# Vector engine instructions in written order from tile 36 on, in an attention and feed-forward kernel

## The chip, the cores and the metric

The kernel runs on one core of one Trainium2 chip. The metric is the device time of one execution in microseconds (us). A core has engines that run side by side, each with its own queue of instructions: TensorE for matmuls and transposes (PE in the profile, with its weight loads as PEld), VectorE (DVE), ScalarE (ACT), GpSimd (POOL) and SyncE (SP), which here issues all DMA transfers. An engine takes its queue from front to back; an instruction that has to wait for another engine holds up what stands behind it in the same queue.

## The reference

```python
# q, k, v: [8, 8, 576, 64]; w_in: [512, 2048]; w_out: [2048, 512]
scores = scale * q @ k.T
thresh = max(scores, axis=-1) - tau
scores = where(scores >= thresh, scores, -1e9)
attn   = exp(scores - max(scores))
attn   = attn / (sum(attn) + 1e-9)
x      = attn @ v                      # heads side by side: [4608, 512]
h      = x @ w_in
out    = (max(h, 0) + log1p(exp(-abs(h)))) @ w_out
```

So it is an attention whose weights below a threshold are dropped, followed by a two-layer feed-forward with softplus between the layers. The matrix products are made in several passes: numbers are split into a high part, rounded to the matmul's format, and a low part, the rest.

## The kernel before

**Tiles.** One unit is one batch with a pair of heads, 32 units in all. A unit has nine tiles of 128 query rows, so there are 288 tiles; the main loop (L924) goes through them one after another. Tiles 0 to 35 are batch 0, and tile 36 is the first of batch 1. A tile of scores is 128 x 576 numbers and lies in one of two pairs of PSUM banks (`SB = 2`).

**A tile's chain.** TensorE makes the scores (L423). DVE takes the negated row maximum `negm` (L430) and the threshold `thr` (L431). ACT makes the exponentials into `e_all` (L435). DVE masks them and sums the rows in the same instruction (L440, `mask`). TensorE transposes the result back into the bank of the scores (L471 to L477). ACT copies the high part `gH` (L498 to L510), and DVE subtracts to get the low part `gL` (L523, L527, both through the helper at L132). TensorE multiplies with v (`values`, L555 to L557); DVE adds the two halves of the result (L566, `xp`). At the end of a unit, DVE makes the reciprocals of the row sums (L571, L572, `rs`), which TensorE transposes (L576, `rT`).

**Feed-forward beside it.** The 4608 rows of x go through the feed-forward in nine chunks of 512. The matmuls of a chunk (L645 to L649 for h, L703 to L707 for the output) are handed out a few at a time between the steps of the tiles, so that TensorE has them while the chain of a tile runs on other engines. A chunk begins when its batch is through the attention. Two finished blocks of h go together through softplus on ACT (L667), which needs another function table than the exponential, so two table loads stand around each pair. From chunk 1 on DVE rounds the result to the high part (L129, `CAST g<-st`, through `hi_of` at L688); POOL subtracts for the low part (L132 on POOL, `g<-st,g`). In chunk 0 ACT does the rounding. The output of 128 rows is made in four quarters of the hidden width, 12 matmuls each; ACT copies the first quarter to `acc` (L718) and DVE adds the other three (L720, `acc<-o,acc`). The blocks of h and o, the products with v, the transposed queries and keys and `rT` share four PSUM banks (`GB = 4`), so a bank is free again only when its reader is done.

**Weights.** w_in and w_out are brought from 64-bit words into 32-bit parts on the core, 32 pieces, one about every two tiles, so from tile 0 to some time after tile 62. A piece is loaded by DMA (L185), goes through ACT (L193) and POOL (L194), then through three integer instructions on DVE (L200, L202, L205, `second`), then POOL. Where there is room (`took > 1`, the pieces named `wa_`), these steps are deferred by some points and each stands behind a mask (`behind(i, masked)`). Where there is none (`took` 0 or 1, the pieces named `ws_`), `later_` calls each step at once, so the three DVE instructions are written directly after the DMA's issue.

**What sets the order.** The code writes a tile's steps by the letters of `PAT`:

```python
PAT = "ThRlefmpfxSvwp"
```

T is the transposes of tile t, h its high parts, R the row maximum of tile t+1, l the low parts of tile t, e the exponentials of t+1, f feed-forward matmuls, m the mask of t+1, x steps of the units beside it, S the scores of t+2, w the next piece of the weights. At p (`point`) the deferred functions that are due are written: softplus one point after its h is complete, the rounding one point after softplus, the sum `acc` and the sum `xp` one point after their matmuls. The written order isn't the order of the queues: when the program is built, the framework's list scheduler lays out each engine's queue with its own estimate of every duration. Among the instructions that it holds for ready it takes the one written first, so an instruction that is ready early goes ahead of one written earlier that still waits. Softplus has a raised priority (`SPP = 150`). `behind(i, others)` adds an edge without a semaphore: it only tells the scheduler that `i` comes after the last of `others`.

Of the kernel before, what the change touches and what calls it, by code (L numbers as in the profile page):

```python
# [59 lines left out]
def tile_kernel(ctx: ExitStack, tc: tile.TileContext, q, k, v, tau, w_in, w_out, out):  # L60
# [89 lines left out]
    def to_f32(src, want, name, then):  # L150
# [47 lines left out]
        def second(n):  # L198
            if n == 0:
                i = nc.vector.tensor_scalar(out=mu, in0=mu, scalar1=3, scalar2=None, op0=ALU.logical_shift_left)  # L200
            elif n == 1:
                i = nc.vector.scalar_tensor_tensor(out=mu, in0=high, scalar=0x80000000, in1=mu,  # L202
                                                   op0=ALU.bitwise_and, op1=ALU.bitwise_or)
            else:
                i = nc.vector.scalar_tensor_tensor(out=mu, in0=low, scalar=29, in1=mu,  # L205
                                                   op0=ALU.logical_shift_right, op1=ALU.bitwise_or)
# [168 lines left out]
    def queries(s, t0, t1, ps):  # L375

        nc.scalar.activation(t0, ps, AF.Copy, scale=qscale)
        if s.i:
            swap(t0, t1)
            return  # L380
        for i, o in ((slice(0, D), slice(D, P)), (slice(D, P), slice(0, D))):
            nc.vector.tensor_scalar(out=t1[o], in0=ps[i], scalar1=qscale[i], scalar2=None, op0=ALU.mult)
# [44 lines left out]
    def row_max(s, t):  # L427
        negm = apool.tile([P, 1], F32, tag="negm", bufs=3, name=f"negm_{s.i}_{t}")
        thr = apool.tile([P, 1], F32, tag="thr", bufs=3, name=f"thr_{s.i}_{t}")
        nc.vector.reduce_max(negm, s.sp[t][:, :, 0:HS], axis=AX.XY, negate=True)  # L430
        nc.vector.tensor_scalar(out=thr, in0=negm, scalar1=-1.0, scalar2=ntau, op0=ALU.mult, op1=ALU.add)  # L431
        s.m[t] = (negm, thr)
# [5 lines left out]
    def mask(s, t):  # L438
        e2 = e_all[:, s.half[t], :].rearrange("p (h n) -> p h n", h=2)
        masked.append(nc.vector.scalar_tensor_tensor(  # L440
# [76 lines left out]
    def weights_lo(s, t):  # L517
# [3 lines left out]
        for g, c0, s0, n in s.place[t]:  # L521
            h, l = group(s, g)
            lo_of(nc.vector, l[:, :, c0:c0 + n], main[:, :, s0:s0 + n], h[:, 0:NC, c0:c0 + n])  # L523
        for x, rows, up, down in rests(s, t):
            for g, c0, s0, n in s.place[x]:
                h = group(s, g)[0]
                lo_of(nc.vector, h[down, NC, c0:c0 + n], rest[rows, s0:s0 + n], h[up, NC, c0:c0 + n])  # L527
# [32 lines left out]
    def values_out(s, g, o):  # L560
# [5 lines left out]
        nc.vector.tensor_tensor(out=xs, in0=o[keep, 0:n], in1=xs, op=ALU.add)  # L566

    def row_scales(s):
        nt = len(s.tiles)
        s.rs = apool.tile([P, 9], F32, tag="rs", name=f"rs_{s.i}")  # L570
        nc.vector.tensor_scalar(out=s.rs[:, 0:nt], in0=s.sums[:, 0:nt], scalar1=1e-9, scalar2=None, op0=ALU.add)  # L571
        nc.vector.reciprocal(s.rs[:, 0:nt], s.rs[:, 0:nt])  # L572
# [104 lines left out]
    def parts_of(u, fc, t):  # L677
# [10 lines left out]
        hi_of(nc.vector if u.n else nc.scalar, gh, t)  # L688
# [23 lines left out]
    def project_out(u, qt, tb, o):  # L712
# [4 lines left out]
        if qt == 0:  # L717
            nc.scalar.copy(a, o)  # L718
        else:
            nc.vector.tensor_tensor(out=a, in0=o, in1=a, op=ALU.add)  # L720
# [66 lines left out]
    now = {"p": 0}  # L787
# [114 lines left out]
    eng, u0.eng, u0.eng_lo = u0.eng, nc.scalar, nc.vector  # L902
# [21 lines left out]
    for g, (cur, t) in enumerate(tiles):  # L924
        t9 = cur.tiles.index(t) + 1
# [73 lines left out]
```

## Time and profile before

| | |
|---|---|
| median of the runs | 1450.6 us (1448.82, 1451.17, 1450.6) |
| profiled execution | 1451.43 us, of which the span is 1449.6 us |
| busy over the span | PE 1398.8, DVE 987.2, ACT 847.1, POOL 590.3 us |
| masks (L440) | 288 of 816 ns |
| row maxima (L430) | 288 of 754 ns |
| roundings (L129) | 128 of 485 ns |
| sums of the output (L720) | 108 of 689 ns |

The profile names an instruction by its line, engine, and output<-inputs. A timeline row is start, duration, engine, line, operation, names, shapes, count, and in brackets the idle time before it with the engine that ended it. A row of waits is the waiting engine and instruction, the engine and instruction waited for, the microseconds in total, how often, and the longest. In a table of windows each engine has its busy time and its number of instructions in that stretch; PEclk is the clock that TensorE was granted, as a share of full speed.

### The profile page before, as it was taken

Reading aid. Unit: us, or ns where it says so; the run is one execution under the profiler, and the core shown is the slowest. Engines: PE = TensorE matmul, PEld = TensorE weight load, DVE = VectorE, ACT = ScalarE, POOL = GpSimd, SP = SyncE. Lnnn points to the kernel's source line nnn. Section 1 sums busy time; section 2 is a strip of 40 time slices with the busy share of each in tenths; the row PEclk is TensorE's granted clock in tenths of the full one; section 3 lists DMA queues with packets and bytes.
Section 4 is the critical chain, followed back from the end, with each engine's and each line's share of the span. In section 5 each row is a group of like instructions: output and inputs, shape, how many; then the busy total and the mean of one; then the engine's idle time right before and its main releaser. Section 6 shows DMA issues by size and latency. Waiting matters only on the chain.

```text
span 1449.6 us, 23487 instructions
## 1 busy us (share of the span) xinstructions
PE 1398.8 (96%) x7860; PEld 1161.8 (80%) x7860; DVE 987.2 (68%) x2211; ACT 847.1 (58%) x1615; POOL 590.3 (41%) x619
## 2 busy tenths in 40 slices
PE   6887999999999999999999999999999999999998
PEld 4555688788888888888888888888888888788886
DVE  6988588787777777777777777777777777402111
ACT  6667667667656576657665665667665765311010
POOL 3667566443333333344334333344334431324221
PEclk9999999999999999999999999999999999999999
DMA  5866765445333533445433533354344432333321
GB/s 170 227 186 206 214 191 182 126 121 160 104 106 114 135 109 116 119 132 151 122 111 96 154 105 100 117 151 120 113 119 135 147 99 73 105 126 130 118 86 44
DMA packets 131208, 189.93 MB, mean 131 GB/s; under 512 B 35312, under 2 KB 86800, under 8 KB 131088
## 3 DMA queue, kind: packets, MB, share of 16 engines
q1 hardware_dynamic: 131088, 188.43, 44.5%
q8 instruction: 63, 1.03, 0.3%
q14 instruction: 57, 0.47, 0.1%
HBM read 140.51 MB, written 27.41 MB: 116 GB/s over the span
## 4 chain that ended last, share of the span: by engine, by line
PE 78%; DVE 8%; ACT 4%; issue 3%; DMA 3%; POOL 3%; SPq 1%; POOLq 0%; DVEq 0%; ACTq 0%
PE s L423 10%; PE h L647 9%; PE h L645 9%; PE h L649 8%; PE o L707 8%; PE o L705 8%; PE o L703 8%; PE s L474 7%; PE pv L555 3%; PE pv L556 3%; PE tr L364 2%; DVE e_all L440 2%; DVE negm L430 2%; POOL g L132 1%; DMA wc_i<-in_moe_w_in_dram 1%
## 5 line engine op out<-in xcount | busy, mean ns | idle before, releaser
L132 POOL TENSOR_TENSOR g<-st,g 128x512 fp32r<-128x512 f32 x144 | 191.6, 1348 | 195.6 <-DVE g L129 184.2
L440 DVE SCALAR_TENSOR_TENSOR e_all<-s,thr,e_all 128x576 f32<-128x576 f32 x288 | 234.6, 816 | 49.1 <-ACT e_all L435 45.8
L430 DVE TENSOR_REDUCE negm<-s 128x1 f32<-128x576 f32 x288 | 217.2, 754 | 43.5 <-PE s L423 36.0
L707 PE MATMUL o<-wo_o,g 128*128 128x512 f32 x576 | 232.5, 404 | 5.3 <-POOL g L132 5.3
L435 ACT ACTIVATE e_all<-s,negm 128x576 f32<-128x576 f32 x288 | 216.0, 750 | 33.5 <-PE tr L471 14.8
L647 PE MATMUL h<-xl,wi 128*128 128x512 f32 x576 | 233.9, 406 | 0.9 <-POOL xl L132 0.9
L703 PE MATMUL o<-wo_o,g 128*128 128x512 f32 x576 | 232.3, 403 | 0.8 <-DVE acc L720 0.4
L645 PE MATMUL h<-xh,wi 128*128 128x512 f32 x576 | 230.6, 400 | 2.3 <-ACT xh L127 2.0
L649 PE MATMUL h<-xh,wi 128*128 128x512 f32 x576 | 230.6, 400 | 0.0
L705 PE MATMUL o<-wo_o,g 128*128 128x512 f32 x576 | 228.4, 397 | 0.0
L498 ACT CAST gH<-s 128x512 fp32r<-128x512 f32 (+1 forms) x270 | 145.1, 550 | 140.6 <-PE s L474 137.8
L132 DVE TENSOR_TENSOR gL<-s,gH 128x512 fp32r<-128x512 f32 (+1 forms) x270 | 169.0, 634 | 46.4 <-ACT gH L498 24.0
L423 PE MATMUL s<-kT,qT 128*128 128x288 f32 x1024 | 193.1, 310 | 7.6 <-ACT gH L512 2.0
L423 PEld LDWEIGHTS s<-kT,qT 128*128 128x128 f32 x1024 | 149.3, 191 | 28.2 <-issue 10.8
L129 DVE CAST g<-st 128x512 fp32r<-128x512 f32 x128 | 57.4, 485 | 149.5 <-ACT st L667 149.0
L474 PE MATMUL s<-identr,e_all 128*128 128x128 f32 x1008 | 154.6, 276 | 3.9 <-DVE e_all L440 3.9
L667 ACT ACTIVATE st<-h 128x512 f32<-128x512 f32 x144 | 78.3, 596 | 115.6 <-PE h L649 115.0
L707 PEld LDWEIGHTS o<-wo_o,g 128*128 128x128 f32 x576 | 108.4, 188 | 29.2 <-POOL g L132 11.0
L474 PEld LDWEIGHTS s<-identr,e_all 128*128 128x128 f32 x1008 | 114.8, 141 | 20.7 <-DVE e_all L440 12.5
L645 PEld LDWEIGHTS h<-xh,wi 128*128 128x128 f32 x576 | 108.9, 189 | 26.1 <-ACT xh L127 2.6
L647 PEld LDWEIGHTS h<-xl,wi 128*128 128x128 f32 x576 | 108.9, 189 | 23.2 <-POOL xl L132 1.7
L649 PEld LDWEIGHTS h<-xh,wi 128*128 128x128 f32 x576 | 109.0, 189 | 21.9
(107 smaller groups left out, 2363.4 us busy)
## 6 DMA issues: line engine op xcount, KB each, us to landing
wi<-wi_d SPq DMA_DIRECT2D x144, 512.0 KB
qT<-qT SPq DMA_DIRECT2D x124, 128.0 KB
R<-r_d SPq DMA_DIRECT2D x64, 144.0 KB
kn<-in_k_dram SPq DMA_DIRECT2D x32, 256.0 KB
qn<-in_q_dram SPq DMA_DIRECT2D x32, 256.0 KB
vn<-in_v_dram SPq DMA_DIRECT2D x32, 256.0 KB
wc_i<-in_moe_w_in_dram SPq DMA_DIRECT2D x16, 512.0 KB
wi_d<-wc_i SPq DMA_DIRECT2D x32, 256.0 KB
```

The source lines that it names most:

```text
L132: eng.tensor_tensor(out=out_, in0=in_, in1=hi.bitcast(F32), op=ALU.subtract)
L423: i = nc.tensor.matmul(sp[:, hf, 0:HS], lhs, s.kT[j][:, k0 + hf * HS:k0 + (hf + 1) * HS], start=(m == 0), stop=(m == len(parts) - 1))
L430: nc.vector.reduce_max(negm, s.sp[t][:, :, 0:HS], axis=AX.XY, negate=True)
L435: nc.scalar.activation(e_all[:, s.half[t], :].rearrange("p (h n) -> p h n", h=2), s.sp[t][:, :, 0:HS], AF.Exp, bias=s.m[t][0], scale=1.0)
L440: masked.append(nc.vector.scalar_tensor_tensor(out=e2, in0=s.sp[t][:, :, 0:HS], scalar=s.m.pop(t)[1], in1=e2, op0=ALU.is_ge, op1=ALU.mult, ...
L474: nc.tensor.matmul(main[:, c, :], e[:, c0:c0 + P], ident, is_transpose=True, start=True, stop=True)
L645: nc.tensor.matmul(h, wi[:, 0, cc, :], u.h[cc], start=(cc == 0), stop=False)
L647: nc.tensor.matmul(h, wi[:, 0, cc, :], u.l[cc], start=False, stop=False)
L649: nc.tensor.matmul(h, wi[:, 1, cc, :], u.h[cc], start=False, stop=(cc == NCC - 1))
L703: nc.tensor.matmul(o, gh[:, sl], wo[fc][:, 0, :], start=(i == 0), stop=False)
L705: nc.tensor.matmul(o, gh[:, sl], wo[fc][:, 1, :], start=False, stop=False)
L707: nc.tensor.matmul(o, gl[:, sl], wo[fc][:, 0, :], start=False, stop=(i == QF - 1))
```

## The change

A class `Queue` wraps the vector engine. From tile 36 on (`now["tile"] >= TG`), every instruction that is issued through it gets an edge without a semaphore behind the one issued before it. All DVE work of the loop goes through the wrapper: row maxima, thresholds, masks, low parts, the sums `xp` and `acc`, reciprocals, roundings and the three steps of the weights. So the DVE queue from there on is the written order, and the scheduler can no longer let one DVE instruction pass another. In it, what is due at the point after a mask stands behind that mask, and ahead of the next row maximum. Nothing is added or removed that runs, no priority is changed, and the queues of the other engines are still laid out by the scheduler, now around another DVE order.

```diff
+    now = {"p": 0, "tile": 0}
...
+    class Queue:
+
+        def __init__(self, eng):
+            self.eng, self.last = eng, []
+
+        def __getattr__(self, name):
+            def call(*args, **kwargs):
+                i = getattr(self.eng, name)(*args, **kwargs)
+                if now["tile"] >= TG:
+                    behind(i, self.last)
+                    self.last = [i]
+                return i
+            return call
+
+    vec = Queue(nc.vector)
...
-                i = nc.vector.tensor_scalar(out=mu, in0=mu, scalar1=3, scalar2=None, op0=ALU.logical_shift_left)
+                i = vec.tensor_scalar(out=mu, in0=mu, scalar1=3, scalar2=None, op0=ALU.logical_shift_left)
...
-        nc.vector.reduce_max(negm, s.sp[t][:, :, 0:HS], axis=AX.XY, negate=True)
+        vec.reduce_max(negm, s.sp[t][:, :, 0:HS], axis=AX.XY, negate=True)
...
-        masked.append(nc.vector.scalar_tensor_tensor(
+        masked.append(vec.scalar_tensor_tensor(
...
-            lo_of(nc.vector, l[:, :, c0:c0 + n], main[:, :, s0:s0 + n], h[:, 0:NC, c0:c0 + n])
+            lo_of(vec, l[:, :, c0:c0 + n], main[:, :, s0:s0 + n], h[:, 0:NC, c0:c0 + n])
...
-        hi_of(nc.vector if u.n else nc.scalar, gh, t)
+        hi_of(vec if u.n else nc.scalar, gh, t)
...
-            nc.vector.tensor_tensor(out=a, in0=o, in1=a, op=ALU.add)
+            vec.tensor_tensor(out=a, in0=o, in1=a, op=ALU.add)
...
     for g, (cur, t) in enumerate(tiles):
+        now["tile"] = g
```

The remaining lines of the diff replace `nc.vector` by `vec` in the same way at L202, L205, L382, L431, L527, L566, L571, L572 and L902.

More of the change, by code (lines that the diff above doesn't have):

```diff
@@ L381, in queries @@
         for i, o in ((slice(0, D), slice(D, P)), (slice(D, P), slice(0, D))):
[L382 removed]
+            vec.tensor_scalar(out=t1[o], in0=ps[i], scalar1=qscale[i], scalar2=None, op0=ALU.mult)
     def swap(t0, t1):
@@ L429, in row_max @@
         thr = apool.tile([P, 1], F32, tag="thr", bufs=3, name=f"thr_{s.i}_{t}")
-        nc.vector.reduce_max(negm, s.sp[t][:, :, 0:HS], axis=AX.XY, negate=True)
-        nc.vector.tensor_scalar(out=thr, in0=negm, scalar1=-1.0, scalar2=ntau, op0=ALU.mult, op1=ALU.add)
+        vec.reduce_max(negm, s.sp[t][:, :, 0:HS], axis=AX.XY, negate=True)
+        vec.tensor_scalar(out=thr, in0=negm, scalar1=-1.0, scalar2=ntau, op0=ALU.mult, op1=ALU.add)
         s.m[t] = (negm, thr)
@@ L526, in weights_lo @@
                 h = group(s, g)[0]
-                lo_of(nc.vector, h[down, NC, c0:c0 + n], rest[rows, s0:s0 + n], h[up, NC, c0:c0 + n])
+                lo_of(vec, h[down, NC, c0:c0 + n], rest[rows, s0:s0 + n], h[up, NC, c0:c0 + n])
     slow, ends = [], []
@@ L565, in values_out @@
         nc.scalar.copy(xs, o[move, 0:n])
-        nc.vector.tensor_tensor(out=xs, in0=o[keep, 0:n], in1=xs, op=ALU.add)
+        vec.tensor_tensor(out=xs, in0=o[keep, 0:n], in1=xs, op=ALU.add)
     def row_scales(s):
@@ L570, in row_scales @@
         s.rs = apool.tile([P, 9], F32, tag="rs", name=f"rs_{s.i}")
-        nc.vector.tensor_scalar(out=s.rs[:, 0:nt], in0=s.sums[:, 0:nt], scalar1=1e-9, scalar2=None, op0=ALU.add)
-        nc.vector.reciprocal(s.rs[:, 0:nt], s.rs[:, 0:nt])
+        vec.tensor_scalar(out=s.rs[:, 0:nt], in0=s.sums[:, 0:nt], scalar1=1e-9, scalar2=None, op0=ALU.add)
+        vec.reciprocal(s.rs[:, 0:nt], s.rs[:, 0:nt])
     def row_scales_T(s):
```

7 lines of the change are left out of this document (3 added, 4 removed).

## The prediction

> **What bounds the kernel now.** First the head of the page, and its chain that ended last.
>
> ```profile
> span 1449.6 us, 23487 instructions
> PE 1398.8 (96%) x7860; PEld 1161.8 (80%) x7860; DVE 987.2 (68%) x2211; ACT 847.1 (58%) x1615; POOL 590.3 (41%) x619
> ...
> PE 78%; DVE 8%; ACT 4%; issue 3%; DMA 3%; POOL 3%; SPq 1%; POOLq 0%; DVEq 0%; ACTq 0%
> ```
>
> TensorE is busy for 96% of the span. The change works on DVE alone, so it can gain only what TensorE still loses to DVE. Where that lies, a table of three stages tells: batch 1, in which the weights are still being prepared; batches 2 to 7; and the two feed-forward chunks at the end.
>
> ```profile
> 145.00:300.00 155.00, 149.44 (x827) 119.25 (x826) 120.89 (x259) 105.05 (x197) 89.49 (x98) 0.98 0.58 170
> 300.00:1250.00 950.00, 939.88 (x5551) 806.47 (x5550) 715.39 (x1646) 614.56 (x1144) 355.41 (x368) 1.00 0.41 120
> 1250.00:1449.60 199.60, 193.92 (x836) 156.20 (x834) 33.60 (x62) 29.24 (x51) 57.43 (x43) 0.99 0.35 107
> ```
>
> The third number is PE, the fifth DVE. TensorE is idle for 5.6 us in the first stage, 10.1 in the second, 5.7 in the last. In the last stage DVE works 33.6 us out of 199.6, so its order hardly matters there, and I cost it at nothing. The waits of TensorE from 145 to 1250 us say who ends the idle time:
>
> ```profile
> PE o L707 <- POOL g L132: 4.3, 11, 0.5
> PE s L474 <- DVE e_all L440: 3.7, 11, 0.4
> ...
> PE s L423 <- DVE gL L132: 1.4, 3, 0.7
> ...
> PE o L703 <- DVE acc L720: 0.4, 1, 0.4
> ```
>
> Two waits come 11 times each, 8.0 us together. Those are what another order of DVE could remove.
>
> **Part 1: a mask no longer stands behind a sum.** One of the 11 waits for a mask, in the timelines of DVE and of TensorE:
>
> ```profile
> 398.88 1.44 DVE L129 CAST g<-st 128x512 fp32r<-128x512 f32 x2 [1.57 <-ACT st L667]
> ...
> 402.14 0.59 DVE L132 TENSOR_TENSOR gH<-s,gH 64x128 fp32r<-64x128 f32 x2
> 402.76 0.69 DVE L720 TENSOR_TENSOR acc<-o,acc 128x512 f32<-128x512 f32 x1
> 403.37 0.81 DVE L440 SCALAR_TENSOR_TENSOR e_all<-s,thr,e_all 128x576 f32<-128x576 f32 x1
> ...
> 407.06 0.17 DVE L571 TENSOR_SCALAR rs<-sums 128x9 f32<-128x9 f32 x1
> ```
> ```profile
> 404.24 0.66 PE L474 MATMUL s<-identr,e_all 128*128 128x128 f32 x4 [0.33 <-DVE e_all L440]
> ...
> 419.62 0.27 PE L576 MATMUL rT<-identr,rs 128*9 128x128 f32 x1
> ```
>
> The sum is written at the point after this mask, but the scheduler let it pass. In written order the mask starts at about 402.76 instead of 403.37, 0.61 us earlier, and the wait of 0.33 us is covered. I take all 3.7 us of this row as gained: **-3.7**. The bounds are -3.7 and 0: the scheduler will also lay the transposes earlier in TensorE's queue, by its own estimate, and what it estimated too short it may estimate too short again.
>
> The sum itself moves behind the mask and its read-out, some 0.9 us here and up to about 2.4 us where it also passes low parts (0.69 and 0.59 us more). What waits for a sum is its PSUM bank. The trace doesn't name banks; but there are four, and TensorE now waits for a sum once, for 0.4 us. A block has 12 matmuls, which at the mean pace of the second stage (950 us over 5551) take 2.1 us, and these are among the longest; so with one other block ahead of the bank's next use a sum may be 2 us late and more. I take 0. The reciprocal (407.06) is also written after the next unit's first mask and goes back some 5 us; its reader, the transpose rT, comes at 419.62, 12.6 us after it: 0.
>
> **Part 2: roundings that stood behind a row maximum go ahead of it.** DVE, POOL and TensorE around one of the 11 waits for POOL:
>
> ```profile
> 469.02 0.76 DVE L430 TENSOR_REDUCE negm<-s 128x1 f32<-128x576 f32 x1 [0.41 <-PE s L423]
> 469.70 0.76 DVE L129 CAST g<-st 128x512 fp32r<-128x512 f32 x2
> ```
> ```profile
> 470.19 2.63 POOL L132 TENSOR_TENSOR g<-st,g 128x512 fp32r<-128x512 f32 x2 [2.39 <-DVE g L129]
> ```
> ```profile
> 471.63 0.50 PE L707 MATMUL o<-wo_o,g 128*128 128x512 f32 x1 [0.50 <-POOL g L132]
> ```
>
> DVE was idle for 0.41 us before the row maximum, and the roundings are written at the point ahead of it. In written order they start up to 0.41 + 0.68 = 1.1 us earlier (as far as softplus is done), POOL was idle and follows at once, and the 0.50 us goes. All 11 waits are of this kind, at the change of a chunk: **-4.0** of the 4.3 (between -4.3 and 0, if softplus is what ends last). The row maximum, its exponentials and mask go back by up to 0.65 us.
>
> **Part 3: roundings behind a mask that waits for ACT.** Here the order costs something. DVE, ACT and TensorE in the first unit of a chunk:
>
> ```profile
> 341.27 0.76 DVE L129 CAST g<-st 128x512 fp32r<-128x512 f32 x2 [1.11 <-ACT st L667]
> 341.94 0.75 DVE L430 TENSOR_REDUCE negm<-s 128x1 f32<-128x576 f32 x1
> ...
> 343.32 0.82 DVE L440 SCALAR_TENSOR_TENSOR e_all<-s,thr,e_all 128x576 f32<-128x576 f32 x1 [0.38 <-ACT e_all L435]
> ...
> 344.09 0.82 DVE L440 SCALAR_TENSOR_TENSOR e_all<-s,thr,e_all 128x576 f32<-128x576 f32 x1
> ```
> ```profile
> 342.55 0.74 ACT L435 ACTIVATE e_all<-s,negm 128x576 f32<-128x576 f32 x1
> ```
> ```profile
> 345.17 0.27 PE L471 MATMUL s<-identr,e_all 128*128 128x128 f32 x1
> ```
>
> ACT did softplus between two table loads first, so the first mask can't start before 343.32. In written order both roundings and the next row maximum stand behind it: roundings at about 344.2 instead of 341.27, row maximum at 344.8 instead of 341.94, and then, through thr and ACT's exponential (0.74 us), the second mask at about 346.5 instead of 344.09, 2.4 us late. Behind it wait the transposes that TensorE now makes at 345.17. Lowest price 0: the scheduler fills the 2.4 us with feed-forward matmuls, as it has done here for the first mask, and TensorE works on. Highest 2.4 us each; with three softplus pairs close together at the start of each of six chunks that is 43 us. I take the low end, because the trace shows such late masks already covered, and 0.05 us each for misfits: **+1**. The roundings' own reader is far off when the chunk has just begun.
>
> [...] First the row: the pair at 398.88 took 1.44 us, the pair at 341.27 took 0.76; POOL was reading and writing SBUF beside the first:
>
> ```profile
> 399.01 1.04 POOL L132 TENSOR_TENSOR vt<-vn,vt 128x320 fp32r<-128x320 f32 x1
> ```
>
> [...]
>
> **Part 4: the weights in batch 1.** The pieces `ws_` are written directly after their DMA, ahead of the row maximum of the next tile. SP, ACT and DVE around the first of the three:
>
> ```profile
> 226.90 0.51 SPq L185 DMA_DIRECT2D wc_o<-in_moe_w_out_dram  x1
> ```
> ```profile
> 232.10 0.67 ACT L193 ACTIVATE ws_o<-wc_o 128x512 f32<-128x512 f32 x1 [0.30 <-DMA wc_o<-in_moe_w_out_dram]
> ```
> ```profile
> 228.99 0.74 DVE L430 TENSOR_REDUCE negm<-s 128x1 f32<-128x576 f32 x1
> ...
> 233.84 0.42 DVE L200 TENSOR_SCALAR ws_o<-ws_o 128x512 uint32<-128x512 uint32 x1
> ...
> 235.50 0.69 DVE L205 SCALAR_TENSOR_TENSOR ws_o<-wc_o,ws_o 128x512 uint32<-128x512 uint32 x1
> ...
> 246.35 0.75 DVE L430 TENSOR_REDUCE negm<-s 128x1 f32<-128x576 f32 x1
> ...
> 254.96 0.43 DVE L200 TENSOR_SCALAR ws_o<-ws_o 128x512 uint32<-128x512 uint32 x1 [0.95 <-POOL ws_o L194]
> ```
>
> In written order the row maximum of 228.99 stands behind the three integer instructions whose data come at 233.84. They take about 1.8 us (L200's 0.42, and L202 taken as L205's 0.69), so it starts at about 235.6, and the tile's chain is 6.6 us late. The second `ws_` piece does it again: the row maximum of 246.35 behind 254.96 + 1.8 = 256.8, at most 10.4 us late, not added to the first but in its place. Behind DVE wait the scores of the next but one tile (their bank is freed by the low parts) and the sums of chunk 0 with their banks. How full the engines are there, and what a gap does to the clock:
>
> ```profile
> 225.00:240.00 15.00, 15.00 (x93) 12.93 (x92) 12.17 (x29) 13.50 (x26) 11.69 (x13) 1.00 0.62 190
> 240.00:255.00 15.00, 15.00 (x90) 12.69 (x89) 13.13 (x30) 9.02 (x19) 11.45 (x13) 1.00 0.44 128
> ```
> ```profile
> 149.00:153.00 4.00, 2.00 (x8) 0.75 (x7) 3.44 (x7) 1.27 (x2) 2.16 (x3) 1.00 0.84 244
> 153.00:157.00 4.00, 3.32 (x10) 2.54 (x11) 1.00 (x4) 1.69 (x4) 3.12 (x3) 0.55 0.73 235
> ```
>
> DVE has 2.8 and 1.9 us of slack in 15, so a delay of 7 us isn't worked off before the next. TensorE has chunk 0 to go on with. The price lies between 0, if chunk 0 covers all of it, and 10.4 us, if nothing does. The two tiles or so that fall back hold some 2 us of TensorE each, which chunk 0's matmuls must replace, while late sums hold one or two of the four banks; I take about a third of the upper end: **+3**. The deferred pieces `wa_` also stand ahead of row maxima, with delays of an instruction or two (0.4 to 0.7 us each), which I count in this.
>
> **The sum.** -3.7 - 4.0 + 1 + 3 = -3.7 us. Against the profiled execution's own 1451.4 (the span 1449.6 and 1.8 around it) that is 1447.7; the median of the runs lies 0.8 below that execution, so **1447 us** as a median.
>
> **The rivals.** (a) *The gain moves with the order.* The scheduler sees masks come earlier, lays the transposes earlier by the same amount, and TensorE waits as before. For it: the layout of TensorE's queue follows DVE's estimated times. Against it: a transpose can't pass matmuls written before it unless something is late. Parts 1 and 2 then give about -2 and part 4 the +3: 1451. (b) *Slower: the weights decide.* DVE stands for the `ws_` pieces, late sums keep banks, and TensorE runs out of chunk 0. It decides once chunk 0 covers less than about a third of the 10.4 us. Price: 10 us, less 3 of gains left elsewhere, and half a clock after a long gap: the rows show 2.00 us of 4.00 idle at 149 and then a clock of 0.55, which over 4 us costs some 2 us. That makes +9, 1460. [...] (c) *Slower in every chunk.* Part 3 isn't covered, and a third of its 43 us appears: +14 with the gains off, about 1461 to 1465; against it speak the late masks that are covered now. (d) *The edges change nothing*, because the order was already the written one: against it stand the rows at 402.76 and 469.70; 1450.6.
>
> **How the numbers follow.** A measurement of this kernel can tell about 0.2% (2.9 us) from no change. The forecast has 0.45, with its own range 1442 to 1450, and four fifths of it lie below 1447.7; (a) 0.21, (b) 0.22, (c) 0.08, (d) 0.04. Faster: 0.36 of the forecast and 0.07 of (a) where more is kept, 0.43. Within 0.2%: 0.09, 0.14 and 0.04, 0.27. Slower: (b) and (c), 0.30. Down to 1440 reach both gains in full (-7.7) with nothing lost and a little more of the first stage's idle time; up to 1460 reaches (b). That leaves out most of (c) and some of the lowest, 0.2 in all.
>
> **What would show it.** Part 1: the wait of L474 for `e_all` is near zero between 300 and 1250 us, and `acc` stands behind the masks. Part 2: the wait of L707 for POOL falls below 1 us. Part 3: masks behind softplus come later, roundings stand behind them, and PE's busy time in that stage stays above 939 us. Part 4: DVE's wait for `ws_o L194` grows from 1.4 us to 7 or more between 225 and 275 us. The forecast is wrong if TensorE's idle time between 145 and 300 us grows by more than 8 us, or if the wait of L474 stays.

## The result, and the profile after

The changed kernel takes **1462.95 us** (median of five runs, 1462.56 to 1465.02), beside 1451.17 us of the kernel before on the same chip. The ratio is 1.0087, with a 95% interval of 1.0074 to 1.0101: slower by 0.9%. The forecast of 1447 us had the wrong sign, and the result lies above its range. In the profiled execution the span went from 1449.6 to 1460.8 us.

In the kernel after, lines below L160 are numbered 17 higher (L423 is L440, L474 is L491, L707 is L724), and every DVE instruction that goes through the wrapper carries line L155. The head of the page and the chain that ended last:

```profile
span 1460.8 us, 23585 instructions
...
PE 1397.6 (96%) x7860; PEld 1167.9 (80%) x7860; DVE 990.8 (68%) x2211; ACT 852.5 (58%) x1615; POOL 587.6 (40%) x619
...
PE 81%; DVE 5%; POOL 4%; ACT 3%; issue 3%; DMA 3%; SPq 0%; POOLq 0%; ACTq 0%; DVEq 0%
```

Work and its busy times are the same, so the page's totals don't say what happened. The table of the three stages does (after; stretch, length, then busy time and count of PE, PEld, DVE, ACT, POOL; then PEclk):

```profile
145.00:300.00 155.00, 137.66 (x751) 109.47 (x749) 113.48 (x231) 99.63 (x185) 85.89 (x93) 0.98 0.56 166
300.00:1250.00 950.00, 940.77 (x5578) 813.97 (x5578) 720.56 (x1659) 621.95 (x1150) 357.39 (x374) 1.00 0.42 120
```

TensorE's idle time in the first stage is 155 - 137.66 = 17.3 us, where it was 5.6. In the second it is 9.2, where it was 10.1. So the loss is in batch 1. Cut finer, first the kernel before, then after:

```profile
145.00:217.00 72.00, 68.56 (x357) 52.24 (x356) 52.17 (x104) 47.97 (x90) 43.55 (x48) 0.95 0.69 203
217.00:300.00 83.00, 80.87 (x472) 67.01 (x472) 68.72 (x156) 57.08 (x107) 45.95 (x51) 1.00 0.48 142
300.00:340.00 40.00, 38.58 (x232) 33.00 (x231) 31.39 (x72) 25.94 (x51) 16.21 (x17) 1.00 0.48 140
```
```profile
145.00:217.00 72.00, 66.98 (x366) 51.35 (x365) 53.27 (x107) 49.45 (x92) 45.55 (x50) 1.00 0.74 221
217.00:300.00 83.00, 70.67 (x387) 58.11 (x385) 60.21 (x125) 50.18 (x93) 40.34 (x44) 0.96 0.40 119
300.00:340.00 40.00, 36.75 (x200) 31.27 (x201) 29.13 (x67) 24.12 (x49) 16.09 (x17) 0.91 0.34 93
```

From 217 to 300 us TensorE is busy for 10.2 us less and issues 387 matmuls instead of 472. Two more things are read here. In the other two stretches it is busy for 1.6 and 1.8 us less. And PEclk is 0.96 and 0.91 where it was 1.00: 4% of 83 and 9% of 40 are up to 6.9 us lost by the clock, where the kernel before lost up to 3.6, between 145 and 217 at 0.95. The sum, 10.2 + 1.6 + 1.8 + 6.9 - 3.6 = 16.9 us, stands beside the 17.6 us that the masks show from tile 0 to tile 80 (-0.9 up to tile 54, and the +18.5 of the table below).

The masks are a clock of their own for this kernel: one for each tile, 288 in all, in the same order in every version. The table gives the time from one tile's mask to another's, from the start times in the trace, and in brackets the difference to before. Tiles 54 to 80 span the stretch with the `ws_` pieces and the start of batch 2, tiles 80 to 284 the later batches but for the last tiles. The last column is the median of the runs.

| version (edges on DVE) | 54 to 80 | 80 to 284 | median, us |
|---|---|---|---|
| before | 113.9 | 901.1 | 1450.1 to 1451.2 |
| after: all, from tile 36 | 132.4 (+18.5) | 893.1 (-8.1) | 1462.95 |
| all, from tile 80 (from80) | 114.5 (+0.5) | 893.0 (-8.2) | 1446.15 |
| all, tiles 36 to 79 (only36to79) | 130.6 (+16.7) | 901.2 (0.0) | 1469.34 |
| as after, weights' steps free (w_free) | 123.3 (+9.3) | 892.9 (-8.2) | 1451.78 |
| as after, only `ws_` steps free (ws_free) | 121.6 (+7.7) | 892.9 (-8.2) | 1456.01 |
| as w_free, sums free until 80 (w_bank_free) | 118.2 (+4.3) | 893.2 (-8.0) | 1449.51 |
| as w_free, low parts free until 80 (w_low_free) | 115.9 (+2.0) | 893.1 (-8.1) | 1446.01 |
| weights, row maxima, masks, 36 to 79 (w_only) | 124.2 (+10.2) | 901.2 (+0.1) | 1462.89 |
| sums behind a mask, from 36 (acc36) | 119.2 (+5.3) | 889.8 (-11.4) | 1442.67 |
| sums behind a mask, from 80 (acc80) | 116.0 (+2.0) | 889.6 (-11.6) | **1439.38** |
| as from80, roundings free (from80_cast) | 114.5 (+0.6) | 891.1 (-10.0) | 1443.48 |
| all, tiles 80 to 283 (mid) | 113.8 (-0.1) | 893.3 (-7.8) | 1443.70 |

Four versions have no edge ahead of tile 80 (from80, acc80, from80_cast, mid). They differ by -0.1 to +2.0 in the first column: that is the scatter of one profiled execution there, and the medians decide where a few microseconds matter. The second column, called the steady one below, holds to some tenths. The change is two effects of opposite sign: some 17 us lost in batch 1, 8 gained after it.

### The profile page after: what moved, and what is told of

The parts are those of the page before. It is cut to its first block, busy times and chain, and to the rows that moved or that the text cites. A ratio compares the mean times of both kernels' runs of the same rounds, so it can differ in the third digit from the quotient of the medians.

```text
span 1460.8 us, 23585 instructions
## 1 busy us (share of the span) xinstructions
PE 1397.6 (96%) x7860; PEld 1167.9 (80%) x7860; DVE 990.8 (68%) x2211; ACT 852.5 (58%) x1615; POOL 587.6 (40%) x619
## 4 chain that ended last, share of the span: by engine, by line
PE 81%; DVE 5%; POOL 4%; ACT 3%; issue 3%; DMA 3%; SPq 0%; POOLq 0%; ACTq 0%; DVEq 0%
PE s L440 10%; PE o L724 9%; PE h L664 8%; PE h L662 8%; PE h L666 8%; PE o L720 8%; PE o L722 8%; PE s L491 7%; PE pv L572 4%; PE pv L573 4%; PE tr L381 2%; DVE e_all L155 1%; DVE negm L155 1%; POOL g L132 1%; PE pv L574 1%
## 5 line engine op out<-in xcount | busy, mean ns | idle before, releaser
L155 DVE SCALAR_TENSOR_TENSOR e_all<-s,thr,e_all 128x576 f32<-128x576 f32 x288 | 235.1, 817 | 75.3 <-ACT e_all L452 71.5
L724 PE MATMUL o<-wo_o,g 128*128 128x512 f32 x576 | 231.7, 404 | 6.6 <-POOL g L132 6.6
L155 DVE TENSOR_REDUCE negm<-s 128x1 f32<-128x576 f32 x288 | 215.1, 747 | 25.6 <-PE s L440 22.5
L155 DVE TENSOR_TENSOR gL<-s,gH 128x512 fp32r<-128x512 f32 (+1 forms) x270 | 168.9, 634 | 68.6 <-ACT gH L515 30.7
L440 PE MATMUL s<-kT,qT 128*128 128x288 f32 x1024 | 191.7, 309 | 12.7 <-DVE gH L155 4.0
L440 PEld LDWEIGHTS s<-kT,qT 128*128 128x128 f32 x1024 | 149.4, 190 | 32.2 <-issue 6.5
L155 DVE CAST g<-st 128x512 fp32r<-128x512 f32 x128 | 55.8, 478 | 145.4 <-ACT st L684 145.4
L491 PE MATMUL s<-identr,e_all 128*128 128x128 f32 x1008 | 153.3, 275 | 0.3 <-DVE e_all L155 0.2
L724 PEld LDWEIGHTS o<-wo_o,g 128*128 128x128 f32 x576 | 108.3, 189 | 30.2 <-POOL g L132 12.1
L662 PEld LDWEIGHTS h<-xh,wi 128*128 128x128 f32 x576 | 108.6, 188 | 27.0 <-ACT xh L127 2.6
L491 PEld LDWEIGHTS s<-identr,e_all 128*128 128x128 f32 x1008 | 119.7, 141 | 12.1 <-DVE e_all L155 2.3
L720 PEld LDWEIGHTS o<-wo_o,g 128*128 128x128 f32 x576 | 109.0, 189 | 24.5 <-ACT qm L413 2.4
```

The source lines that it names most:

```text
L155: i = getattr(self.eng, name)(*args, **kwargs)
L440: i = nc.tensor.matmul(sp[:, hf, 0:HS], lhs, s.kT[j][:, k0 + hf * HS:k0 + (hf + 1) * HS], start=(m == 0), stop=(m == len(parts) - 1))
L491: nc.tensor.matmul(main[:, c, :], e[:, c0:c0 + P], ident, is_transpose=True, start=True, stop=True)
L662: nc.tensor.matmul(h, wi[:, 0, cc, :], u.h[cc], start=(cc == 0), stop=False)
L720: nc.tensor.matmul(o, gh[:, sl], wo[fc][:, 0, :], start=(i == 0), stop=False)
L724: nc.tensor.matmul(o, gl[:, sl], wo[fc][:, 0, :], start=False, stop=(i == QF - 1))
```

## Experiments

**Where the loss and the gain lie: from80 and only36to79.** The edges are put on in one part of the loop alone.

```diff
-                if now["tile"] >= TG:
+                if now["tile"] >= 80:              # from80
+                if TG <= now["tile"] < 80:         # only36to79
```

> The edges begin at tile 80 in place of 36, so batch 1 has its old order. Theory A (the loss lies in batch 1, where the written order makes DVE stand for the weights; from tile 80 on the order gains): the changed kernel falls 17.6 us behind up to tile 80 and then wins 8 us back, so without the first part the time is about 8 us below the kernel before, 1443. Theory B (the written order costs wherever it holds, and the late start of batch 2 is only where it shows): a loss of some microseconds stays, 1452 to 1460. Theory C (the gain after tile 80 is only the making up of a delay, as feed-forward work done ahead of its time is then missing from the queue): no change against before, 1450 to 1452.

> The edges hold from tile 36 to 79 only. Theory A: the loss of 17.6 us at tile 80 stays and nothing is won back, 1468 to 1470. Theory C (the gain after tile 80 comes by itself once a delay is there): 1462 to 1463, as in the changed kernel.

from80 took 1446.15 us, ratio 0.9961 (0.9946 to 0.9976); only36to79 1469.34 us, ratio 1.0125 (1.011 to 1.0141). The loss stays whole when the later edges are gone, and the gain stays whole when the earlier edges are gone. So the gain is no making up of lost time, and the two parts can be studied one by one. only36to79 is where theory A put it; from80 is 3 us above the 1443 of theory A, and 1.6 of them are lost again behind the last mask (run mid, below). By the medians the two parts are -4.7 and +18.5 us, together +13.7; the change as a whole measured +11.8. Runs of one kernel differ by 2 us and more, so sums of medians agree no better than that.

**What loses in batch 1: w_free and ws_free.** The three integer steps of the weights go around the chain of edges, all of them or those of the `ws_` pieces alone.

```diff
         def second(n):
+            eng = nc.vector                               # w_free
+            eng = vec if took > 1 else nc.vector          # ws_free
             if n == 0:
-                i = vec.tensor_scalar(out=mu, in0=mu, scalar1=3, ...
+                i = eng.tensor_scalar(out=mu, in0=mu, scalar1=3, ...
...
```

> The edges begin at tile 36, but the three integer instructions of the weights are left out of the chain of edges, all pieces alike. Theory A1 (DVE stands for pieces whose data are not there): the loss up to tile 80 falls from 17.6 us to below 4, time 1443 to 1447. Theory A2 (what hurts in batch 1 is that sums, low parts and row maxima can't pass each other while PSUM banks are scarce): the loss stays above 10 us, 1453 to 1462.

> As the one before, but only the three pieces without room (ws_, whose steps are written directly after their DMA) are left out of the chain; the deferred pieces stay in it. If the waits for ws_ (5.9 us of DVE's idle time in the changed kernel) are the cause: 1445 to 1449, the loss at tile 80 below 6 us. If the deferred pieces, which stand ahead of row maxima with 1.4 to 3.4 us for two of their instructions, are the cause: 1456 to 1462.

w_free took 1451.78 us, ratio 1.0005 (0.9995 to 1.0016), ws_free 1456.01 us, ratio 1.0029 (1.0017 to 1.0042). Against the 1462.95 of the change, freeing the `ws_` steps gives 6.9 us and the `wa_` steps another 4.2: 11.2 us for the weights. But 1451.78 misses the 1443 to 1447 that the theory of the weights alone expected. 5.6 us are still missing to from80's 1446.15. And 1456.01 is at the lower end of what was expected if the deferred pieces were the cause (1456 to 1462), and far from the other theory: the `ws_` pieces are the larger share, and not the whole.

**The weights by themselves: w_only.** The other way round: between tiles 36 and 79 only the weights' steps, the row maxima with their thresholds, and the masks are chained; all else is left to the scheduler.

```diff
-                if now["tile"] >= TG:
+                if TG <= now["tile"] < 80:
...
-            vec.tensor_tensor(out=a, in0=o, in1=a, op=ALU.add)
+            nc.vector.tensor_tensor(out=a, in0=o, in1=a, op=ALU.add)
...
```

(The same for low parts, `xp`, roundings, the row scales and the scaling of the transposed queries.)

> From tile 36 to 79 only the weights' three steps, the row maxima and the masks are chained in written order; sums, casts, low parts and the rest are left to the scheduler; no chain from tile 80 on. Theory V (the weights' steps cost what they cost because the row maximum and the mask of the next tile stand behind them): 8 us or more lost between masks 54 and 80, and 1457 to 1463 at the end. Theory U (the row maxima alone behind the weights are covered by chunk 0; the loss needs the low parts and the sums in the same queue): under 5 us lost, 1450 to 1455.

1462.89 us, ratio 1.0091 (1.0074 to 1.0107): theory V, and at the upper end of it. These few edges lose 12.8 us by the medians (10.2 in the first column of the profile) and gain nothing later. The trace shows the mechanism in one piece. DVE, ACT and TensorE of w_only at the second `ws_` piece:

```profile
253.50 0.69 DVE L737 TENSOR_TENSOR acc<-o,acc 128x512 f32<-128x512 f32 x1
257.52 0.43 DVE L155 TENSOR_SCALAR ws_o<-ws_o 128x512 uint32<-128x512 uint32 x1 [3.32 <-POOL ws_o L211]
257.98 1.42 DVE L155 SCALAR_TENSOR_TENSOR ws_o<-wc_o,ws_o 128x512 uint32<-128x512 uint32 x2
259.31 0.75 DVE L155 TENSOR_REDUCE negm<-s 128x1 f32<-128x576 f32 x1
...
260.87 0.82 DVE L155 SCALAR_TENSOR_TENSOR e_all<-s,thr,e_all 128x576 f32<-128x576 f32 x1 [0.56 <-ACT e_all L452]
```
```profile
256.12 0.67 ACT L210 ACTIVATE ws_o<-wc_o 128x512 f32<-128x512 f32 x1 [2.60 <-DMA wc_o<-in_moe_w_out_dram]
```
```profile
255.97 0.40 PE L666 MATMUL h<-xh,wi 128*128 128x512 f32 x1
261.75 0.48 PE L488 MATMUL s<-identr,e_all 128*128 128x128 f32 x1 [5.39 <-DVE e_all L155]
```

Read from below: TensorE has done all that stands ahead in its queue, the last of it feed-forward, and stands for 5.39 us. It waits for a mask, the mask waits for the exponentials, they for the row maximum at 259.31, and that stands in DVE's queue behind the `ws_` steps. Those wait for POOL, POOL for ACT, and ACT for a DMA. The scores of this row maximum had been there for 5 us or more: this is the last row of scores ahead of the stop.

```profile
253.05 0.74 PE L440 MATMUL s<-kT,qT 128*128 128x288 f32 x4
```

A load from memory has come into the chain of a tile. Right after, the clock falls: the two windows around this place in w_only.

```profile
255.00:260.00 5.00, 1.36 (x6) 0.75 (x4) 2.42 (x4) 0.67 (x1) 2.64 (x4) 0.93 0.35 102
260.00:265.00 5.00, 2.57 (x10) 1.99 (x11) 3.91 (x12) 2.93 (x5) 1.98 (x3) 0.50 0.21 82
```

TensorE is busy for 3.9 us of 10 here, and 2.6 of them run at half clock, which makes them worth 1.3.

**What is left without the weights: w_bank_free and w_low_free.** Both start from w_free and also let something else pass until tile 80: the sums `acc` and `xp`, which free the four banks of TensorE's other products, or the low parts, which free the bank of the scores.

```diff
-            vec.tensor_tensor(out=a, in0=o, in1=a, op=ALU.add)
+            (vec if now["tile"] >= 80 else nc.vector).tensor_tensor(out=a, in0=o, in1=a, op=ALU.add)   # w_bank_free; xp alike
...
-            lo_of(vec, l[:, :, c0:c0 + n], main[:, :, s0:s0 + n], h[:, 0:NC, c0:c0 + n])
+            lo_of(vec if now["tile"] >= 80 else nc.vector, l[:, :, c0:c0 + n], main[:, :, s0:s0 + n], h[:, 0:NC, c0:c0 + n])   # w_low_free; the other half alike
```

> The change without the weights' three steps, and until tile 80 also without what empties PSUM banks of other products than scores: acc (sums of the output) and xp (second half of the attention output). Theory K (the 7.0 us at mask 80 that are left without the weights come from banks that sums hold longer): the loss at mask 80 falls from 7.0 to 0 to 2.5 us, the time is 1443 to 1447. Theory L (they come from low parts, which free the scores' bank, standing behind masks that wait for ACT): the loss stays at 5 to 8 us, 1450 to 1453.

> The change without the weights' three steps, and until tile 80 also without the low parts (gL and gH from the scores' bank). Theory L (low parts behind masks that wait for ACT free the scores' bank late): the loss at mask 80 falls from 7.0 to 0 to 2.5 us, the time is 1443 to 1447. Theory K (banks held by sums): the loss stays at 5 to 8 us, 1450 to 1453. If both this and the run without the bank-emptying sums stay above 4 us at mask 80, neither instruction alone is the cause.

w_low_free took 1446.01 us, ratio 0.9966 (0.995 to 0.9981), as much as from80, so all 5.6 us are back. w_bank_free took 1449.51, ratio 0.9985 (0.9973 to 0.9998): 2.3 us are back, and by its time neither theory is met. The profile of w_bank_free misleads here: from mask 0 to mask 80, where theory K asked for a loss of 0 to 2.5 us, it shows 1.0 (w_low_free 1.5, w_free 7.0), but that execution was the fastest of ten, 1446.03 us, without any half clock behind the start. By the medians the low parts in the chain account for all of the rest, and the sums for part of the same.

How a low part costs TensorE time is not shown. Theory L named the wait of the scores for their bank, and the trace of after has such waits from 145 to 300 us:

```profile
PE s L440 <- DVE gL L155: 4.2, 3, 1.6
...
PE s L440 <- DVE gH L155: 2.1, 1, 2.1
```

The scores (L440) wait 6.3 us for low parts (`gL`, `gH`), where the kernel before has 1.4 in the same stretch. But in w_free, without the weights, these waits are 3.6 us, and in w_low_free, with the low parts out of the chain, they are still 3.8. So by these profiles, what the edit of w_low_free gives back does not come from this wait. For the sums, the run acc36 below has them alone.

**What gains after batch 1: acc80 and from80_cast.** acc80 has no chain at all; each sum of the output gets one edge, behind the last mask that is written ahead of it. from80_cast is from80 with the roundings left out of the chain.

```diff
-    vec = Queue(nc.vector)
+    vec = nc.vector                                       # acc80
...
-            vec.tensor_tensor(out=a, in0=o, in1=a, op=ALU.add)
+            i = nc.vector.tensor_tensor(out=a, in0=o, in1=a, op=ALU.add)
+            if now["tile"] >= 80:
+                behind(i, masked)
```
```diff
-        hi_of(vec if u.n else nc.scalar, gh, t)
+        hi_of(nc.vector if u.n else nc.scalar, gh, t)     # from80_cast, on top of from80
```

> No chain of edges; from tile 80 each sum of the output (acc) alone stands behind the last mask written ahead of it, every other DVE instruction is left to the scheduler. Theory P (the gain from tile 80 on is part 1 of the prediction, masks no longer behind a sum): the lead at mask 284 over the kernel before is 7 to 9 us as with the whole chain from tile 80 (8.1), the wait of L474 for e_all is gone, the time is 1443 to 1446. Theory Q (the gain needs the order of the other instructions too, casts, row maxima, low parts): less than half of it, 1447.5 to 1451.

> The chain from tile 80 on, with the roundings of the feed-forward tiles (CAST g<-st) left out of it. Theory A (the casts' place is worth nothing, because the scheduler lays the o matmuls earlier with them, rival a for part 2): 1446 within 1.5 us, the wait of L707 for POOL stays near 5 us either way. Theory B (the earlier casts are part of the gain): 1448 to 1450.5.

acc80 took **1439.38 us**, ratio 0.9923 (0.99 to 0.9946), better than either theory allowed: one edge per sum gains 11.6 us between tiles 80 and 284, and the whole chain 8.2. from80_cast took 1443.48, ratio 0.9947 (0.9924 to 0.9969), with -10.0 in the steady column. So part 1 is more than the whole gain; keeping the roundings in the chain takes 1.8 us of it back, and the rest of the chain 1.6. Neither theory of from80_cast saw that sign; the lower of them ended at 1444.5. Here is the place of acc80 that answers to the mask of 403.37 in the prediction:

```profile
401.42 1.44 DVE L129 CAST g<-st 128x512 fp32r<-128x512 f32 x2 [1.57 <-ACT st L684]
...
405.30 0.82 DVE L457 SCALAR_TENSOR_TENSOR e_all<-s,thr,e_all 128x576 f32<-128x576 f32 x1
...
406.04 0.69 DVE L737 TENSOR_TENSOR acc<-o,acc 128x512 f32<-128x512 f32 x1
```
```profile
406.29 0.60 PE L491 MATMUL s<-identr,e_all 128*128 128x128 f32 x4
```

The sum is behind its mask, which starts 3.88 us after the rounding where it was 4.49 before (403.37 - 398.88): the 0.61 us that the prediction worked out for it. The transposes at 406.29 have no idle time in front of them. The rounding of 1.44 us beside them still stands where the scheduler puts it. From 300 to 1200 us, the kernel before and then acc80:

```profile
300.00:1200.00 900.00, 890.17 (x5274) 764.44 (x5273) 678.67 (x1562) 589.14 (x1098) 348.78 (x363) 1.00 0.42 122
```
```profile
300.00:1200.00 900.00, 894.68 (x5331) 775.85 (x5330) 686.53 (x1582) 592.90 (x1109) 349.93 (x364) 1.00 0.41 123
```

Idle time falls by 4.5 us (9.8 to 5.3), but TensorE gets through 57 more matmuls, 1.1% of 900 us or some 10 us. So a part of the waiting was inside "busy": a feed-forward matmul is shown for 0.39 us, and the next one starts 0.24 us after it (rows of after at 259.17 and 259.41 below), so the first 0.15 us of a delay don't show as idle time. The starts tell more. The distances from the start of an output matmul to the transposes that follow it, where they exceed the usual distance of that pair, add up to 5.5 us in eleven cases before, between tiles 80 and 284; the view of waits gave 3.7. In acc80 they are gone. Measured in the same way, the distances from a transpose of keys or queries to the scores behind it hold 4.0 us more than usual before and 0.3 in acc80, and those from `rT` to the scores 1.3 and about 0; these are delays of 0.1 to 0.2 us each. The three are some 10.4 of the 11.6 us; what held up the scores in the latter two wasn't tried.

**Sums alone in batch 1: acc36.** As acc80, with the edge from tile 36 on.

```diff
-            if now["tile"] >= 80:
+            if now["tile"] >= TG:
                 behind(i, masked)
```

> As the run with the sums alone behind the last mask, but from tile 36 on, so through batch 1 too. Theory K (in batch 1 late sums hold banks and cost TensorE time by themselves): a loss of 2 us or more between masks 54 and 80, 1441.5 to 1445. Theory L (a late sum alone costs nothing there as long as low parts and weights are free): within 1 us at mask 80, 1438 to 1441.

1442.67 us, ratio 0.9946 (0.9926 to 0.9966): 3.3 us more than acc80, with which it shares the steady column (-11.4). That is in the range of theory K, but the intervals of the two runs overlap, and acc80's own profile has +2.0 of scatter in the same tiles. That late sums cost something in batch 1 is likely; how much isn't settled, nor why nothing of it is left in w_low_free, which has the same sums in its chain.

**The end: mid.** The whole chain from tile 80 to tile 283 only.

```diff
-                if now["tile"] >= TG:
+                if 80 <= now["tile"] < 284:
```

> The whole chain from tile 80 to 283, none in the last unit and after it. Theory E (the chain takes back 1.6 us after the last mask, where the row scales and the second halves of the attention output stand behind other DVE work): 1444 to 1445.5, against 1446.2 with the chain up to the end. Theory F (the end only differs by chance): 1446 to 1447.5.

1443.70 us, ratio 0.9956 (0.9939 to 0.9973), against 1446.15 with the chain up to the end: on the side of theory E, but with overlapping intervals. The profiles settle it: in the profiled execution of from80 the lead over before falls from 8.0 us at the last mask to 6.4 at the end of the span, and in mid it stays at 8.9. All seven versions with the chain up to the end lose 1.5 to 3.2 us against before in that stretch, and the five without it 0.1 at most. Which instruction there costs it isn't shown. The prediction's "I cost it at nothing" for the last stage is off by 1.5 us in after.

## Why the prediction was wrong, step by step

**Part 4, the weights: the step that failed.** The mechanism was named as it is (row maxima behind `ws_` steps that wait for data); its size was not: +3 was taken between 0 and 10.4, and the weights in written order cost 12.8 us alone (w_only) and 11.2 within the change. Four things went wrong in the sizing.

First, the upper bound. It was the delay of one row maximum, "at most 10.4 us late, not added to the first but in its place". That row maximum, at 246.35 us before, starts at 260.01 in after: 13.7 us late. The one ahead of it was 4.8 us late already (247.28 instead of 242.44). And a row maximum behind a piece waits for a transfer, and the transfer has no fixed time: it moves back with the tiles. The loads in SP's queue, before and then after:

```profile
237.80 0.40 SPq L185 DMA_DIRECT2D wc_o<-in_moe_w_out_dram  x1
248.46 0.33 SPq L185 DMA_DIRECT2D wc_o<-in_moe_w_out_dram  x1
```
```profile
225.03 0.34 SPq L202 DMA_DIRECT2D wc_o<-in_moe_w_out_dram  x1
...
241.44 0.53 SPq L202 DMA_DIRECT2D wc_o<-in_moe_w_out_dram  x1
...
253.28 7.12 SPq L202 DMA_DIRECT2D wc_o<-in_moe_w_out_dram  x2
```

The first load was issued at 226.90 before (quoted in the prediction) and is issued at 225.03 now, earlier by 1.9 us; the second (of a `wa_` piece) comes at 241.44 instead of 237.80, and the third (of the second `ws_` piece) at 253.28 instead of 248.46, later by 3.6 and 4.8. So the delays do add: what came late after the first `ws_` piece made the second one's data late too. DVE of after at that piece, and ACT ahead of it:

```profile
251.83 1.42 DVE L155 SCALAR_TENSOR_TENSOR wa_o<-wc_o,wa_o 128x512 uint32<-128x512 uint32 x2
258.21 0.43 DVE L155 TENSOR_SCALAR ws_o<-ws_o 128x512 uint32<-128x512 uint32 x1 [4.96 <-POOL ws_o L211]
258.67 1.42 DVE L155 SCALAR_TENSOR_TENSOR ws_o<-wc_o,ws_o 128x512 uint32<-128x512 uint32 x2
260.01 0.75 DVE L155 TENSOR_REDUCE negm<-s 128x1 f32<-128x576 f32 x1
```
```profile
256.82 0.66 ACT L210 ACTIVATE ws_o<-wc_o 128x512 f32<-128x512 f32 x1 [1.43 <-DMA wc_o<-in_moe_w_out_dram]
```

DVE stands for 4.96 us at once; the wait for `ws_o` in all grew from 1.4 to 5.9 us, where the prediction asked for 7 or more. That test, read alone, would have said that the mechanism is smaller than thought. It isn't, because TensorE's loss is larger than DVE's wait: the row maximum at 260.01 takes its exponentials, mask, transposes and low parts with it.

Second, the cover. "TensorE has chunk 0 to go on with" was true for the first microseconds after each stop and not beyond: in w_only the queue of TensorE ended with a matmul at 255.97, and then came 5.39 us of nothing. TensorE takes its queue in order too: the next feed-forward matmul there started at 264.14, behind the transposes of 261.75 and 262.02, and didn't cover for them.

Third, the clock, which was priced at 2 us in the rival (b) alone. In after it costs up to the 6.9 us worked out above, 3.3 more than before in the same stretch. Two of the four places in which it fell, and four matmuls around the second:

```profile
245.00:250.00 5.00, 2.54 (x17) 1.91 (x16) 3.98 (x10) 3.23 (x6) 2.82 (x4) 1.00 0.26 70
250.00:255.00 5.00, 4.85 (x20) 4.42 (x21) 3.15 (x7) 1.78 (x4) 1.57 (x2) 0.66 0.38 99
...
260.00:265.00 5.00, 2.03 (x12) 1.52 (x11) 4.49 (x11) 2.24 (x6) 2.58 (x4) 0.97 0.32 105
265.00:270.00 5.00, 5.00 (x24) 4.35 (x24) 4.82 (x12) 1.10 (x3) 2.12 (x3) 0.69 0.23 59
```

```profile
259.17 0.39 PE L662 MATMUL h<-xh,wi 128*128 128x512 f32 x1
259.41 0.39 PE L664 MATMUL h<-xl,wi 128*128 128x512 f32 x1
...
266.15 0.63 PE L666 MATMUL h<-xh,wi 128*128 128x512 f32 x1
266.57 0.63 PE L662 MATMUL h<-xh,wi 128*128 128x512 f32 x1
```

Here the two stretches in which TensorE is about half idle (busy for 2.54 and 2.03 us of 5) are followed by one at a mean clock of 0.66 and one at 0.69. From one feed-forward matmul to the next it takes 0.42 us there, and 0.24 ahead of the pause. So these gaps were paid for twice.

Fourth, the deferred pieces `wa_`. They were counted in, with 0.4 to 0.7 us of delay each; the runs give them 4.2 us (ws_free against w_free). In after the first of the late row maxima (227.48 instead of 223.60) stands behind no `ws_` piece but behind a `wa_` pair of 3.35 us, which the last section shows.

**What part 4 didn't price: the low parts.** The prediction mentioned that the scores' bank is freed by low parts and gave it no price of its own. Low parts in the chain cost 5.6 us once the weights are out of it (w_free against w_low_free and from80); that it goes by the scores' bank is not shown.

**Part 1, masks ahead of sums: right in mechanism, too small.** The wait of L491 for `e_all` is gone between 300 and 1250 us, as foretold. -3.7 was predicted; alone the edge is worth -11.6 between tiles 80 and 284 (acc80). The mis-sized term is the price of one such wait. It was taken from the view of waits, which shows only the idle part: 3.7 us, where the starts of the transposes were 5.5 us late in all. Some 5 us more were lost at scores, away from these waits, and are gone with the same edge; by what way is open.

**Part 2, roundings ahead of row maxima: wrong.** -4.0 was predicted, and none of it came: roundings in the chain, which is parts 2 and 3 together, are a small loss of 1.8 us by the steady column. The wait of L724 for POOL stays. TensorE's waits in after, from 300 to 1250 us:

```profile
PE o L724 <- POOL g L132: 5.6, 11, 0.7
```

Before, it was 4.3 us in 11 waits from 145 to 1250, and with the roundings out of the chain it is 4.3 in 11 again (from80_cast). Nor are all 11 of one kind: ten are, two at each of five changes of a chunk, and the one at 313.4 us belongs to chunk 0, where ACT does the rounding. The place from the prediction (rounding at 469.70, matmul at 471.63) is best measured from the mask ahead of it, which in the kernel before is this one:

```profile
467.79 0.82 DVE L440 SCALAR_TENSOR_TENSOR e_all<-s,thr,e_all 128x576 f32<-128x576 f32 x1
```

The same place in from80, on DVE, POOL and TensorE:

```profile
466.15 0.82 DVE L155 SCALAR_TENSOR_TENSOR e_all<-s,thr,e_all 128x576 f32<-128x576 f32 x1
...
467.86 0.76 DVE L155 CAST g<-st 128x512 fp32r<-128x512 f32 x2 [0.89 <-ACT st L684]
468.53 0.75 DVE L155 TENSOR_REDUCE negm<-s 128x1 f32<-128x576 f32 x1
```
```profile
468.36 2.63 POOL L132 TENSOR_TENSOR g<-st,g 128x512 fp32r<-128x512 f32 x2 [1.08 <-DVE g L155]
```
```profile
469.81 0.51 PE L724 MATMUL o<-wo_o,g 128*128 128x512 f32 x1 [0.73 <-POOL g L132]
```

The rounding did go ahead of the row maximum, but it starts 1.71 us after the mask where it was 1.91: 0.2 us earlier and not 1.1, because now it waits 0.89 us for softplus. That is the bound of 0 that the prediction named ("if softplus is what ends last"), and it is what holds. The matmul comes 3.66 us after the mask instead of 3.84 and waits 0.73 us instead of 0.50, so the queue of TensorE was laid earlier by somewhat more than POOL is, as the rival (a) said. And the row maximum pays: 2.38 us after the mask instead of 1.23. The prediction counted up to 0.65 us for that and gave it no price.

**Part 3, roundings behind masks that wait for ACT: its direction was right.** DVE's waits for the exponentials from 330 to 1200 us are the sign of it, before and after:

```profile
DVE e_all L440 <- ACT e_all L435: 26.0, 47, 0.9
```
```profile
DVE e_all L155 <- ACT e_all L452: 45.5, 40, 3.2
```

The longest went from 0.9 to 3.2 us, with the roundings behind it. +1 was predicted. The 1.8 us of the roundings hold parts 2 and 3 together, and the whole chain costs 11.6 - 8.2 = 3.4 us against the sums alone. So part 3 wasn't measured by itself, its order of magnitude is right, and (c)'s 14 us are out.

**The sum** by the runs: about +17 in batch 1 (1462.95 against from80's 1446.15), -4.7 for all that lies behind it, +12 in all. Of the rivals (b) came nearest, with DVE that stands for the pieces and with its 1460, but also with 10 us as the whole price, 7 too little. The late sums that it named beside them aren't needed: w_only has the sums outside the chain and loses 12.8 us. The prediction's own test for being wrong, an idle time from 145 to 300 us that grows by more than 8, was met with 11.8.

## What to carry to other kernels

An order written by hand is worth no more than its worst member: before an in-order edge is laid on an engine, list which of its instructions wait for a DMA or for a long chain on other engines, and leave those out. The gain here was in one kind of instruction (a sum that nobody waited for in those batches, put behind a mask that TensorE waits for); one edge for each gave more than the chain of all, 1439.38 against 1446.15 us, and beats both kernels. Bound such an edge's cost by what stands behind the instruction on its engine, with the wait repeated as often as it comes and the clock that a gap can take with it (up to 6.9 us in after), and not by a single delay.

## What the runs showed of the hardware

The two integer instructions of a piece (two inputs each) took from 1.42 to 3.35 us as a pair in one execution of after. There, on DVE and on POOL:

```profile
224.21 3.35 DVE L155 SCALAR_TENSOR_TENSOR wa_o<-wc_o,wa_o 128x512 uint32<-128x512 uint32 x2
```
```profile
224.02 2.99 POOL L132 TENSOR_TENSOR g<-st,g 128x512 fp32r<-128x512 f32 x2 [5.64 <-ACT g L127]
```

The pair takes 3.35 us beside POOL's subtraction, and 1.42 at 251.83, where POOL is idle from 249.57 to 253.34. The prediction had 0.69 for each, from a row of the kernel before. Of the five pairs of after between 224 and 261 us, the three beside a POOL instruction with two inputs took 3.35, 2.52 and 3.33 us, and the two beside an idle POOL 1.42 each: 4.9 us more of DVE's time in all. What makes a pair beside POOL longer isn't shown. No run took this cost alone away, so its share of the loss isn't measured; in written order the scheduler can't put the pair where POOL is quiet.

The half-clock stretches in the clock records of before and after, from 30 to 1240 us, are 3.41 and 6.83 us long in before and four times 3.41 us in after. Cut both traces there into stretches of 3.41 us at the times where the clock changes, and take those at full clock. All three in which TensorE was busy for 45% or less (43 and 41% in before, 39% in after) were followed by half clock, three of 11 with 46 to 64% (49, 55 and 63%, all in after), and none of the rest, some 690. The same pause did not always cost clock: before, a pause of 2.0 us that ended at 153.0 us fell into one stretch (41% busy), and 6.8 us at half clock followed (PEclk 0.95 from 145 to 217 us); in after the same pause falls into two (60 and 58%), and the clock stays (1.00). 3.4 us at half clock are worth up to 1.7 us, about the scatter of the first column.
